# A fixed order of 218 dense chains and a new set of 82 split exponentials in an attention and state-space kernel

## The chip, the cores and the metric

The kernel runs on one core of a Trainium2 chip. The metric is device time in microseconds (us) of one execution. One execution of each kernel is recorded by the profiler; the others are only timed.

A "burst" is one of 512 equal attention steps, and its length is the time from the start of its first exponential on ScalarE to the start of the next burst's first. I compare sums over bursts 17 to 510.

## The reference, cut to what matters

```python
x = A_x                                          # 2048 tokens x 1024
g = sigmoid((x * gate_w).sum(-1, keepdims=True))
a = state_space(x, ...)                          # h[t] = Lam*h[t-1] + B x[t];  y = 2 Re(C h) + x * Dskip
b = attention(x, wqkv, wo)                       # 32 heads of 32, softmax over 2048 keys
return g * a + (1 - g) * b
```

## The kernel before

The two branches run through each other. The attention is the frame: bursts of eight score matmuls, two exponentials of 128x1024 and some sixteen 33-column matmuls of the attention-value product for earlier bursts. Everything else on TensorE (projections "p", state-space inputs "u", state-space outputs "c", the output product "o") is cut into 218 chains that accumulate in one PSUM bank, number 7. A chain has mostly 8 or 16 units, a unit being one 512-column matmul or its like; a burst takes four units. A python function lays the program out once, at build time, and keeps its own rough clock for that.

In some bursts (the set `DVB`) the first exponential is split: ScalarE does a 128x512 half, VectorE the other half in five operations (exp_a to exp_f). I call these bursts "halves".

```python
DVB_FROM = 69
DVB_NOT = (69, 73, 77, ..., 389, 457)           # cut: 34 numbers
DVB = {B for B in range(69, 508) if B % 4 == 1 and B not in DVB_NOT}      # 76 halves (condensed)

def exp(self, B, z, s):
    ...
    if z == 0 and B in DVB:
        self.dve_exp(B, s, p)                    # ScalarE 128x512, VectorE exp_a now, exp_b to exp_f queued in self.dx
    else:
        self.act(lambda e: e.activation(self.tile[p], ps[:, 2 * s:2 * s + 2, :], ACT.Exp, scale=SCALE), ...)

# score buffers: three pairs of PSUM banks in turn
sl = [(2 * self.p) % 3, (2 * self.p + 1) % 3]

# attention-value quarters (four matmuls each) that a burst may take
cap = 5
if p in DVB or p + 1 in DVB:
    cap = 3

# units of dense work in burst p
quota = 3 if p in DVB else 5 if p + 1 in DVB and ... else 4      # condensed

# the next chain: a greedy choice (cut to its core)
if n_ok and left <= need + 4:        cur = nxt.pop(0)            # projection that is due
elif c_ok and ...:                   cur = cs.pop(0)[1]
elif u_ok:                           cur = us.pop(0)[3]
elif c_ok:                           cur = cs.pop(0)[1]
elif n_ok:                           cur = nxt.pop(0)

# a state-space output chain: 16 units, plus four 128x128 matmuls that count as 0 units
for q in range(4):
    mms.insert(5 * q + 3, (0, lambda e, f, l, ...: e.matmul(ps[:, 7, 128 * q:128 * (q + 1)], xT[...], self.diagD[:, dt, :], ...)))

# VectorE's queue: exponential operations first, one after the other
def fill(self, limit):
    while True:
        for src in (self.dx, self.bg, self.bg2):
            ...
```

## Time and profile before

931.95 us, median of 3 (931.95 to 932.35); the profiled execution spans 930.6 us. The busy table of the page (busy us, share of the span, instructions; PE is TensorE's matmuls, PEld its weight loads, DVE VectorE, ACT ScalarE, POOL GpSimd):

```profile
PE 916.7 (99%) x15316; PEld 528.4 (57%) x15316; DVE 733.3 (79%) x1349; ACT 914.9 (98%) x1034; POOL 8.9 (1%) x39
```

Two engines seem full. TensorE's busy time does not tell where it sets the pace: in a stretch that ScalarE paces, shown below, TensorE is busy 29.30 of 29.33 us. (The records of its matmuls overlap: one of 512 columns lasts 0.38 us, and the next of its chain starts 0.215 us after it.) The chain of waits shows which of the two sets the pace where. The first fence is a piece of it between bursts 150 and 152, among halves in every fourth burst; the columns are start, duration and what (L1651 scores, L1725 attention-value, L1481 and L1487 a state-space output chain).

```profile
285.05 0.33 PE f_ps L1651 x8
285.38 0.60 PE f_ps L1725 x20
285.98 0.66 PE f_ps L1481 x3
286.64 0.06 PE f_ps L1487
286.70 0.22 PE f_ps L1481
286.91 0.33 PE f_ps L1651 x8
```

The second is from a stretch without halves (bursts 273 to 288).

```profile
506.71 0.87 PE f_ps L1452 x4
507.58 0.46 PE f_ps L1651 x8
508.04 0.30 PE f_ps L1725 x8
508.34 0.87 PE f_ps L1452 x4
509.21 0.19 PE f_ps L1725 x8
509.41 0.47 PE f_ps L1651 x8
```

In the first, eight score matmuls take 0.33 us and TensorE goes straight from one thing to the next: TensorE paces, and the trace has the first exponential of each burst from 145 to 160 starting about 40 ns after its scores end (from 273 to 288 it is 71 ns or more in 14 of 16 bursts). In the second the same eight take 0.46 us: they wait in the middle for a score buffer that ScalarE has not yet emptied (by the timeline the first such group begins at 507.51 and its third matmul at 507.65, the exponential that reads this buffer having ended at 507.60; the view of waits has 1.7 us of `PEld f_ps L1651 <- ACT f_pt L1667` in bursts 273 to 288 and none in 145 to 160). ScalarE paces. The windows view shows the two kinds side by side; I chose the windows to begin and end at the start of a burst's first exponential, 16 bursts each (145 to 160 first, then 273 to 288), and the column to read is the first number, the length.

```profile
276.83:305.25 28.42, 28.42 (x470) 15.75 (x467) 25.13 (x43) 28.35 (x33) 0.00 (x0) 1.00 0.13 44
500.72:530.05 29.33, 29.30 (x514) 18.35 (x515) 28.02 (x49) 29.33 (x33) 0.27 (x2) 1.00 0.20 43
```

| what (start to next start, or a fit over bursts where the exponential waits for its scores) | us |
|---|---|
| exponential 128x1024 on ScalarE: best, and mean where ScalarE paces | 0.903, 0.917 |
| half exponential 128x512 on ScalarE | 0.494 |
| scores and fixed part of a burst on TensorE (fit) | 0.502 |
| one 33-column matmul, one 512-column, one 128-column (fit) | 0.024, 0.208, 0.053 |
| VectorE, 512 columns, reading the result of the operation before / not reading it | 0.725 / 0.603 |

Over bursts 17 to 510 (8124 33-column, 1735 512-column and 1024 128-column matmuls, 76 halves) the values of the table give TensorE 858 us of work and ScalarE 861 us at its best, and the trace has 878.2 us.

### The profile page before, as it was taken

What the parts mean: (1) busy time and instruction counts of PE and PEld (TensorE: products, weight loads), DVE (VectorE), ACT (ScalarE), POOL (GpSimd) and SP (SyncE); (2) the same over time, 40 slices, a digit from 0 to 9 for tenths busy, and PEclk for the clock granted to TensorE, in tenths of its full rate; (3) what the DMA queues carried; (4) which work ended last, traced back from release to release, by engine and by line L of the source; (5) the groups of instructions that cost most, each with busy time, mean ns of one, the idle gap of its engine ahead of it and who ended that gap; (6) DMA issues with size and microseconds to landing.
All of it is one profiled execution on the core that took longest, in us unless ns stands there. A gap on an engine that the chain in (4) does not pass through costs nothing.

```text
span 930.6 us, 33709 instructions
## 1 busy us (share of the span) xinstructions
PE 916.7 (99%) x15316; PEld 528.4 (57%) x15316; DVE 733.3 (79%) x1349; ACT 914.9 (98%) x1034; POOL 8.9 (1%) x39
## 2 busy tenths in 40 slices
PE   8999999999999999999999999999999999999996
PEld 4555755557555565555655755555655556555553
DVE  2799979999988888886699966579889565766775
ACT  6999999999999999999999999999999999999996
POOL 2000000000000000000000000000000000000000
PEclk9999999999999999999999999999999999999998
DMA  9559433310431004101033201233110212233322
GB/s 204 104 84 154 79 53 76 73 30 5 87 62 42 30 6 86 52 29 31 19 73 63 43 16 56 62 62 72 32 41 8 73 53 93 100 87 123 116 64 75
DMA packets 157076, 60.90 MB, mean 65 GB/s; under 512 B 145664, under 2 KB 145664, under 8 KB 156928
## 3 DMA queue, kind: packets, MB, share of 16 engines
q1 hardware_dynamic: 154768, 58.16, 28.0%
q8 instruction: 121, 1.98, 0.9%
q10 hardware_dynamic: 2160, 0.53, 0.3%
q14 instruction: 27, 0.22, 0.1%
HBM read 16.79 MB, written 12.58 MB: 32 GB/s over the span
## 4 chain that ended last, share of the span: by engine, by line
PE 61%; ACT 36%; DVE 1%; SPq 1%; DMA 1%; issue 0%; DVEq 0%
ACT f_pt L1667 32%; PE f_ps L1725 17%; PE f_ps L1651 13%; PE f_ps L1452 9%; PE f_ps L1481 9%; PE f_ps L1422 8%; PE f_ps L1440 4%; ACT f_ub L1692 1%; SPq L1076 1%; ACT f_wb L1692 1%; DMA f_xT<-in_A_x_dram 1%; ACT f_Et L1667 1%; ACT f_cT_re L1667 1%; PE f_ps L1487 1%; ACT f_cT_im L1667 0%
## 5 line engine op out<-in xcount | busy, mean ns | idle before, releaser
L1667 ACT ACTIVATE f_pt<-f_ps 128x1024 bf16<-128x1024 f32 x868 | 817.7, 1227 | 0.6 <-PE f_ps L1651 0.6
L1725 PEld LDWEIGHTS f_ps<-f_V,f_pt 128*128 128x128 bf16 x6944 | 240.4, 96 | 136.0 <-issue 97.6
L1725 PE MATMUL f_ps<-f_V,f_pt 128*128 128x33 bf16 x6944 | 293.7, 178 | 0.0
L1651 PE MATMUL f_ps<-f_Q,f_K 32*128 32x256 bf16 x4096 | 225.5, 274 | 3.4 <-ACT f_cT_re L1667 1.2
L1651 PEld LDWEIGHTS f_ps<-f_Q,f_K 32*128 32x128 bf16 x4096 | 75.6, 92 | 120.2 <-ACT f_pt L1667 53.5
L1452 PE MATMUL f_ps<-f_xT,f_wb 128*128 128x512 bf16 x512 | 131.0, 377 | 0.9 <-DVE f_pf L1247 0.6
L1422 PE MATMUL f_ps<-f_xT,f_wb 128*128 128x512 bf16 x464 | 119.0, 378 | 0.0
L1371 DVE TENSOR_TENSOR_SCAN f_ht<-f_pf,f_init,f_ut 128x512 bf16<-128x512 f32 x64 | 80.6, 1273 | 0.0
L1481 PE MATMUL f_ps<-f_cT_im,f_hp 128*128 128x512 bf16 x192 | 72.6, 378 | 0.0
L1481 PE MATMUL f_ps<-f_cT_re,f_hp 128*128 128x512 bf16 x192 | 72.5, 378 | 0.0
L1693 DVE TENSOR_SCALAR f_wb<-f_ps 128x512 int32<-128x512 f32 x47 | 32.5, 691 | 49.1 <-PE f_ps L1651 48.7
L1512 PE MATMUL f_ps<-f_wb,f_OT 128*128 128x512 bf16 x252 | 65.9, 380 | 0.0
L1440 PE MATMUL f_ps<-f_wb,f_xT 128*128 128x128 bf16 x896 | 59.1, 219 | 0.0
L1452 PEld LDWEIGHTS f_ps<-f_xT,f_wb 128*128 128x128 bf16 x512 | 40.2, 96 | 32.4 <-issue 0.7
L1422 PEld LDWEIGHTS f_ps<-f_xT,f_wb 128*128 128x128 bf16 x464 | 36.2, 96 | 28.2
L1440 PEld LDWEIGHTS f_ps<-f_wb,f_xT 128*128 128x128 bf16 x896 | 50.4, 97 | 0.1
L1458 DVE CAST f_ub<-f_ps 128x512 bf16<-128x512 f32 x48 | 33.0, 687 | 14.6 <-PE f_ps L1452 14.3
L1363 DVE TENSOR_TENSOR f_tq<-f_ht,f_Et 128x1024 bf16<-128x1024 bf16 x64 | 42.0, 684 | 0.2
L1363 DVE TENSOR_TENSOR f_ut<-f_tq 128x512 f32<-128x512 bf16 x64 | 41.9, 683 | 0.0
L1494 DVE TENSOR_SCALAR f_Ag<-f_ps,f_gcol 128x512 f32<-128x512 f32 x32 | 24.0, 751 | 13.0 <-PE f_ps L1481 12.6
L1700 DVE SCALAR_TENSOR_TENSOR f_Ag<-f_Ag,f_wb 128x512 f32<-128x512 f32 x47 | 32.5, 691 | 1.4
L1692 ACT ACTIVATE f_wb<-f_ps 128x512 bf16<-128x512 f32 x47 | 33.3, 709 | 0.2
(160 smaller groups left out, 937.7 us busy)
## 6 DMA issues: line engine op xcount, KB each, us to landing
ag_scratch<-f_Ag SPq DMA_DIRECT2D x32, 256.0 KB, 2.4
f_hp<-ag_scratch SPq DMA_DIRECT2D x32, 256.0 KB, 3.0
f_wb<-in_B_wqkv_dram SPq DMA_DIRECT2D x21, 256.0 KB, 3.7
out_dram<-f_xT SPq DMA_DIRECT2D x16, 256.0 KB, 2.1
f_wb<-in_B_wo_dram SPq DMA_DIRECT2D x1, 1024.0 KB, 5.3
f_OT<-f_On SPq DMA_TRANSPOSE x63, 2.3
f_wb<-in_B_wo_dram SPq DMA_DIRECT2D x1, 768.0 KB, 6.6
f_wb<-in_B_wqkv_dram ACTq DMA_DIRECT2D x2, 256.0 KB, 4.1
```

The lines of the kernel that those rows point to most:

```text
L1363: ops.append((c, lambda: dve(lambda e: e.tensor_tensor(o, a, b, op), r, w() if callable(w) else w)))
L1371: ops.append((1.192, lambda ri=ri: dve(lambda e: e.tensor_tensor_scan(ht[:, ri, :], rr, ut[:, ri, :], self.init[:, ri, j:j + 1], ALU.mult, ...
L1422: mms.append((1, lambda e, f, l, a=a: e.matmul(ps[:, bank, :], w[:, g % 2, part, a, :], xT[:, a, 512 * ch:512 * (ch + 1)], start=f, stop=l ...
L1440: m = e.matmul(ps[:, bank, 128 * q:128 * (q + 1)], xT[:, a, 128 * kt:128 * (kt + 1)], w[:, g % 2, 2, a, :], start=(a == 0), stop=(a == 7))
L1452: mms.append((1, lambda e, f, l, a=a: e.matmul(ps[:, 7, :], bT[:, n % 2, ri, a, :], xT[:, a, 512 * ch:512 * (ch + 1)], start=f, stop=l), [ ...
L1458: self.dve(lambda e: e.tensor_copy(self.ub[k][:, ri, :], ps[:, 7, :]), [("bank", 7)], [("ub", k, ri)] + over, "evac_u")
L1481: mms.append((1, lambda e, f, l, j=j, ri=ri: e.matmul(ps[:, 7, :], hp[:, ri, j, cols], cT[ri][:, j, 512 * cb:512 * (cb + 1)], start=f, sto ...
L1512: mms.append((1, lambda e, f, l, j=j: e.matmul(ps[:, 7, :], OT[:, j, 256 * qb + 128 * r:256 * qb + 128 * (r + 1)], wo[j][0][:, 512 * cb:51 ...
L1651: m = e.matmul(ps[:, 2 * sl[z] + h % 2, 256 * kl:256 * (kl + 1)], K[32 * h:32 * h + 32, g % 2, 128 * kt:128 * (kt + 1)], Q[32 * h:32 * h + ...
L1667: self.act(lambda e: e.activation(self.tile[p], ps[:, 2 * s:2 * s + 2, :], ACT.Exp, scale=SCALE), [("S", s)], [("pt", p)], "exp")
L1692: self.S.op("act", lambda e: e.activation(t[:, 0, :], ps[:, 2 * s, :], ACT.Exp, scale=SCALE), reads=[("S", s)], writes=[("pt", p)], deps=d ...
L1725: m = e.matmul(ps[:, 6, o:o + 33], self.tile[p][:, h2, 256 * kl + 128 * qt:256 * kl + 128 * (qt + 1)], V[:, g % 2, 2 * i + kl, h, :], star ...
```

## The change

The intent: let a search on a timing model choose the order of all dense chains and the set of halves together, and write both down as lists. To make room on VectorE, exponential operations are interleaved with others (a dependent operation then does not follow its source directly), and some small VectorE operations become fewer and larger.

```diff
-DVB_FROM = 69
-DVB_NOT = (69, 73, 77, ... 457)
+ORDER = "".join(w[0] * int(w[1:]) for w in (
+    "u2 p2 u4 p1 u2 p2 u2 p9 u8 p1 ... p1 c1 p2 c1 p2 c1 p1 u4 c1 u2 p1 c1 p2 c1 u2 p4 c1 p2 c1 u2 p3 ..."   # cut
+    "... p9 c5 p1 c3 u4 ... u2 p9 c8 p3 o36 ").split())
+DVB_RUNS = ((109, 113), (129, 177), (185, 257), (277, 277), (285, 329), (345, 345), (365, 381), (389, 453), (461, 505))
+DVB = {B for lo, hi in DVB_RUNS for B in range(lo, hi + 1, 4)}
...
-                    if n_ok and left <= need + 4:
-                        cur = nxt.pop(0)
-                    elif ...                                     # the greedy choice, cut
+                    kind = order[0]
+                    ...                                          # is the next one of this kind ready?
+                    if not ok:
                         break
+                    order.pop(0)
+                    cur = take()
...
-            for src in (self.dx, self.bg, self.bg2):
+            for src in self.sources():
...
+        if self.dx:
+            out.insert(1 if self.last_dx and self.p < self.dx_due else 0, self.dx)
...
 # fold of C: 64 operations of 512 columns become 32 of 1024; tables: 32 products become 16;
 # the copy of a scan's last column moves behind two other operations
```

The set gains 109, 113, 129, 133, 257, 277, 285, 345, 381, 389 and loses 181, 269, 353, 361: 76 halves become 82.

More of the change, by code (lines that the diff above doesn't have):

```diff
@@ L936 @@
 MM_PER_PERIOD = 4
+UB4 = 16
+DEP = 0.122
 EXP_A = 16713.9646930418
@@ L941 @@
 EXP_C0 = 3607248267949745.0
-DVB_FROM = 69
-DVB_NOT = (69, 73, 77, 81, 85, 89, 93, 97, 101, 105, 109, 113, 117, 121, 125, 129, 133, 257, 261, 265, 273, 277, 281, 285, 333, 337, 341, 345, 349, 357, 381, 385, 389, 457)
-def dve_bursts():
-    return [B for B in range(DVB_FROM, 508) if B % 4 == 1 and B not in DVB_NOT]
-DVB = set(dve_bursts())
+ORDER = "".join(w[0] * int(w[1:]) for w in (
+    "u2 p2 u4 p1 u2 p2 u2 p9 u8 p1 u1 p1 u1 p1 u1 p1 u1 p1 u1 p1 u1 p1 c1 p2 c1 p2 c1 p1 u4 c1 u2 p1 c1 p2 c1 u2 p4 c1 p2 c1 u2 p3 u2 c2 u1 c6 u1 p12 u4 "
+    "p1 u2 p1 u4 p9 c5 p1 c3 u4 p1 u2 p1 u2 p1 u4 p1 u2 p8 u2 p9 c8 p3 o36 ").split())
+DVB_RUNS = ((109, 113), (129, 177), (185, 257), (277, 277), (285, 329), (345, 345), (365, 381), (389, 453), (461, 505))
+DVB = {B for lo, hi in DVB_RUNS for B in range(lo, hi + 1, 4)}
 REST = 508
@@ L1315, in diag_d, with fold_ops @@
                       ["ident", ("pf", 3)], [("diagD", j)])
-    def fold_ops(self, j, cb):
+    def fold_ops(self, j):
         pf = self.pf
         a1, a2, b2 = pf[:, self.A1, j:j + 1], pf[:, self.A2, j:j + 1], pf[:, self.B2, j:j + 1]
-        X, Y = self.fold[:, 0:512], self.fold[:, 512:1024]
-        cols = slice(512 * cb, 512 * cb + 512)
-        cr, ci = self.cT[0][:, j, cols], self.cT[1][:, j, cols]
+        X, Y = self.fold[:, 0:1024], self.fold[:, 1024:2048]
+        cr, ci = self.cT[0][:, j, :], self.cT[1][:, j, :]
         q = lambda *i: [("pf", k) for k in i]
-        gp = ["gp%d" % i for i in range(4)] if j == cb == 0 else []
-        return [(0.4, lambda: self.dve(lambda e: e.tensor_scalar(X, ci, a2, None, ALU.mult), [("cT", 1, j)] + q(self.A2), ["fX"] + gp)),
-                (0.4, lambda: self.dve(lambda e: e.tensor_scalar(Y, cr, a2, None, ALU.mult), [("cT", 0, j)] + q(self.A2), ["fY"])),
-                (0.66, lambda: self.dve(lambda e: e.scalar_tensor_tensor(cr, cr, a1, X, ALU.mult, ALU.add), [("cT", 0, j), "fX"] + q(self.A1), [("cTf", 0, j, cb)])),
-                (0.66, lambda: self.dve(lambda e: e.scalar_tensor_tensor(ci, ci, b2, Y, ALU.mult, ALU.add), [("cT", 1, j), "fY"] + q(self.B2), [("cTf", 1, j, cb)])),
+        gp = ["gp%d" % i for i in range(4)] if j == 0 else []
+        return [(0.66, lambda: self.dve(lambda e: e.tensor_scalar(X, ci, a2, None, ALU.mult), [("cT", 1, j)] + q(self.A2), ["fX"] + gp)),
+                (0.66, lambda: self.dve(lambda e: e.tensor_scalar(Y, cr, a2, None, ALU.mult), [("cT", 0, j)] + q(self.A2), ["fY"])),
+                (1.196, lambda: self.dve(lambda e: e.scalar_tensor_tensor(cr, cr, a1, X, ALU.mult, ALU.add), [("cT", 0, j), "fX"] + q(self.A1), [("cTf", 0, j)])),
+                (1.196, lambda: self.dve(lambda e: e.scalar_tensor_tensor(ci, ci, b2, Y, ALU.mult, ALU.add), [("cT", 1, j), "fY"] + q(self.B2), [("cTf", 1, j)])),
                 (0.0, lambda: self.folded.append(j))]
@@ L1335, in table_ops @@
         EF, Et, prod = self.EF, self.Et, self.fold.rearrange("p (k a b) -> p k a b", k=4, a=32)
-        lo = [EF[:, r, 16 * j:16 * (j + 1)].unsqueeze(1).to_broadcast([128, 32, 16]) for r in range(2)]
-        hi = [EF[:, r, 128 + 32 * j:160 + 32 * j].unsqueeze(2).to_broadcast([128, 32, 16]) for r in range(2)]
+        lo = EF[:, :, 16 * j:16 * (j + 1)].unsqueeze(2).to_broadcast([128, 2, 32, 16])
+        lor = EF[:, ::-1, 16 * j:16 * (j + 1)].unsqueeze(2).to_broadcast([128, 2, 32, 16])
+        hi = EF[:, :, 128 + 32 * j:160 + 32 * j].unsqueeze(3).to_broadcast([128, 2, 32, 16])
         first = ["m_a0", "m_a1", "m_a2", "m_k", "m_h", "m_y", "m_s"] if j == 0 else []
@@ L1341, in table_ops @@
         ops = []
-        for k, (x, y) in enumerate(((0, 0), (1, 1), (0, 1), (1, 0))):
-            ops.append((0.6, lambda k=k, x=x, y=y: self.dve(lambda e: e.tensor_tensor(prod[:, k], hi[x], lo[y], ALU.mult), self.EFtok, ["gp%d" % k] + (first if k == 0 else []))))
+        for k, y in ((0, lo), (2, lor)):
+            ops.append((1.136, lambda k=k, y=y: self.dve(lambda e: e.tensor_tensor(prod[:, k:k + 2], hi, y, ALU.mult), self.EFtok,
+                                                         ["gp%d" % k, "gp%d" % (k + 1)] + (first if k == 0 else []))))
         for r, op in ((0, ALU.subtract), (1, ALU.add)):
@@ L1372, in item_ops @@
                                                 [("ut", ri), "init", ("pf", self.RR)], [("ht", ri)])))
+        tt(0.602, tq[:, 0:2, :], ht[:], E2, ALU.mult, [("ht", 0), ("ht", 1), Et], [("tq", 0)])
+        tt(0.602, tq[:, 2:4, :], ht[:], E2r, ALU.mult, [("ht", 0), ("ht", 1), Et], [("tq", 2)])
         if ch < 3:
             ops.append((0.19, lambda: dve(lambda e: e.tensor_copy(self.hl[:, :, j], ht[:, :, 511]), [("ht", 0), ("ht", 1)], [("hl", j)])))
-        tt(0.602, tq[:, 0:2, :], ht[:], E2, ALU.mult, [("ht", 0), ("ht", 1), Et], [("tq", 0)])
-        tt(0.602, tq[:, 2:4, :], ht[:], E2r, ALU.mult, [("ht", 0), ("ht", 1), Et], [("tq", 2)])
         hw = ["warm"] if ch == 0 and j == 0 else []
@@ L1466, in ub_of @@
     def ub_of(self, n):
-        return n % 4 if n < 16 else n % 2
+        return n % 4 if n < UB4 else n % 2
     def done_item(self, n):
@@ L1481, in d_c @@
                 mms.append((1, lambda e, f, l, j=j, ri=ri: e.matmul(ps[:, 7, :], hp[:, ri, j, cols], cT[ri][:, j, 512 * cb:512 * (cb + 1)], start=f, stop=l),
-                            [("hp", b, j, ri), ("cTf", ri, j, cb)]))
+                            [("hp", b, j, ri), ("cTf", ri, j)]))
         for q in range(4):
@@ L1697, in dve_exp @@
         self.waiting.add(B)
-        self.dx += [(0.45, lambda: self.dve(lambda e: e.tensor_scalar(hi, hi, 0.0, 128.0, ALU.max, ALU.mult), [I], [I], "exp_b")),
-                    (0.69, lambda: self.dve(lambda e: e.scalar_tensor_tensor(xw, lo, EXP_C2, lo, ALU.add, ALU.mult), [I], [W], "exp_c")),
-                    (0.69, lambda: self.dve(lambda e: e.scalar_tensor_tensor(xw, xw, EXP_C1, lo, ALU.add, ALU.mult), [I, W], [W], "exp_d")),
-                    (0.69, lambda: self.dve(lambda e: e.scalar_tensor_tensor(t[:, 1, :], xw, EXP_C0, ev, ALU.add, ALU.mult), [I, W], [("ptd", p)], "exp_f")),
+        self.last_dx, self.dx_due = True, B + 3
+        self.dx += [(0.365, lambda: self.dve(lambda e: e.tensor_scalar(hi, hi, 0.0, 128.0, ALU.max, ALU.mult), [I], [I], "exp_b")),
+                    (0.603, lambda: self.dve(lambda e: e.scalar_tensor_tensor(xw, lo, EXP_C2, lo, ALU.add, ALU.mult), [I], [W], "exp_c")),
+                    (0.603, lambda: self.dve(lambda e: e.scalar_tensor_tensor(xw, xw, EXP_C1, lo, ALU.add, ALU.mult), [I, W], [W], "exp_d")),
+                    (0.603, lambda: self.dve(lambda e: e.scalar_tensor_tensor(t[:, 1, :], xw, EXP_C0, ev, ALU.add, ALU.mult), [I, W], [("ptd", p)], "exp_f")),
                     (0.0, lambda: self.waiting.discard(B))]
@@ L1745, in normalize @@
             if g == 3:
-                assert self.items_done >= 16
+                assert self.items_done >= UB4
                 x += [("ub", k, ri) for k in (2, 3) for ri in range(2)]
@@ L1762, in build @@
         self.holds, self.left_in = {}, {}
+        self.last_dx, self.dx_due = False, 0
         self.dx, self.seen_x, self.waiting, self.x_now, self.busy_w = [], set(), set(), None, None
@@ L1791, in build @@
                 for tq in range(4):
-                    cs.append((ch, self.d_c(ch, tq, cb, len(cs)), 8 + 8 * cb))
+                    cs.append((ch, self.d_c(ch, tq, cb, len(cs))))
         self.c_left = [8, 8, 8, 8]
@@ L1807, in build @@
         cur = None
+        order = list(ORDER)
         first = FIRST
@@ L1840, in build @@
                 self.normalize(nq // 32 - 1)
+                self.last_dx = False
                 self.dve_t = max(self.dve_t, rn) + 0.6
@@ L1845, in build @@
                 if nc == 8:
-                    for cb in range(2):
-                        for j in range(8):
-                            self.bg2 += self.fold_ops(j, cb)
+                    for j in range(8):
+                        self.bg2 += self.fold_ops(j)
             while self.later and self.later[0][0] <= p:
@@ L1878, in build @@
                 if cur is None:
-                    if ended is not None:
+                    if ended is not None or not order:
                         break
-                    if proj[0] and p >= FIRST + 4:
-                        cur = proj[0].pop(0)
-                    elif not last:
-                        nxt = proj[g + 1]
-                        left = 64 - pg
-                        need = 2 * len(nxt)
-                        u_ok = c_ok = False
-                        if us:
-                            ch, n, ri, dn = us[0]
-                            hp_free = ch < 2 or (ch == 2 and self.c_left[0] == 0) or (ch == 3 and self.c_left[2] == 0)
-                            u_ok = ri == 1 or (self.items_done >= n - (3 if n < 18 else 1) and hp_free)
-                        if cs:
-                            c_ok = self.items_done >= 8 * (cs[0][0] + 1) and p > self.item_p + 1 and len(self.folded) >= cs[0][2]
-                        n_ok = nxt and pg >= nxt[0].after
-                        if n_ok and left <= need + 4:
-                            cur = nxt.pop(0)
-                        elif c_ok and cs[0][0] == 1 and p + 4 * sum(self.c_left[:2]) + need >= 254:
-                            cur = cs.pop(0)[1]
-                        elif u_ok:
-                            cur = us.pop(0)[3]
-                        elif c_ok:
-                            cur = cs.pop(0)[1]
-                        elif n_ok:
-                            cur = nxt.pop(0)
-                    elif outs and p >= outs[0][0]:
-                        cur = outs.pop(0)[1]
@@ L1907, in build @@
-                    if cur is None:
+                    kind = order[0]
+                    if kind == "p":
+                        if proj[0]:
+                            ok, src = p >= FIRST + 4, proj[0]
+                        else:
+                            src = proj[g + 1] if g + 1 < GROUPS else None
+                            ok = src and pg >= src[0].after
+                        take = lambda: src.pop(0)
+                    elif kind == "u":
+                        ch, n, ri, dn = us[0]
+                        hp_free = ch < 2 or (ch == 2 and self.c_left[0] == 0) or (ch == 3 and self.c_left[2] == 0)
+                        ok = ri == 1 or (self.items_done >= n - (3 if n < UB4 + 2 else 1) and hp_free)
+                        take = lambda: us.pop(0)[3]
+                    elif kind == "c":
+                        ok = self.items_done >= 8 * (cs[0][0] + 1) and p > self.item_p + 1 and len(self.folded) == 8
+                        take = lambda: cs.pop(0)[1]
+                    else:
+                        ok = last and p >= outs[0][0]
+                        take = lambda: outs.pop(0)[1]
@@ L1935, in build @@
                 ended.evac()
+                self.last_dx = False
                 st = max(self.dve_t, ready)
@@ L1939, in build @@
         self.log = log
-        assert not outs and cur is None and nq == 4 * NBURST - 8
+        self.missing = sum(w for w in [dn.left for dn in [cur] if dn]) + sum(dn.left for l in (us, cs, outs) for dn in [t[3] if len(t) == 4 else t[1] for t in l])
+        assert not self.missing and nq == 4 * NBURST - 8
         self.tail()
@@ L1945, in fill @@
         while True:
-            for src in (self.dx, self.bg, self.bg2):
-                if not src:
-                    continue
-                if src is self.bg:
-                    n = src[0][2]
-                    if n < 8 and n not in self.tabled or n >= 8 and len(self.folded) < 16:
-                        continue
-                if src is self.bg2 and len(src[0]) > 2 and self.p < src[0][2]:
-                    continue
+            for src in self.sources():
                 c = src[0][0]
+                if src is self.dx and self.last_dx:
+                    c += DEP
                 if c == 0 or self.dve_t + c <= limit:
@@ L1958, in fill @@
                     self.dve_t += c
+                    if c:
+                        self.last_dx = src is self.dx
                     break
@@ L1961, in fill, with sources @@
                 return
+    def sources(self):
+        out = []
+        for src in (self.bg, self.bg2):
+            if not src:
+                continue
+            if src is self.bg:
+                n = src[0][2]
+                if n < 8 and n not in self.tabled or n >= 8 and len(self.folded) < 8:
+                    continue
+            if src is self.bg2 and len(src[0]) > 2 and self.p < src[0][2]:
+                continue
+            out.append(src)
+        if self.dx:
+            out.insert(1 if self.last_dx and self.p < self.dx_due else 0, self.dx)
+        return out
     def tail(self):
```

## The prediction

> **What bounds the kernel now.** The busy table shows TensorE 99%, ScalarE 98%, VectorE 79%, clock 0.996. [...] I read the rhythm of the exponentials in the timeline. A burst gives ScalarE two 128x1024 exponentials; in 76 bursts the first is a 128x512 half (start to next start 0.49 us), VectorE doing the other half.
>
> - In stretches without halves (bursts 65 to 128, 257 to 288, 337 to 352) ScalarE paces: 29.33 us per 16 bursts, 0.917 us per exponential, 0.903 at best. A fit of burst lengths where ScalarE waits for the scores puts TensorE's work there at 27.5 to 28.0 us (about 0.50 us of scores, 0.024 us per 33-column matmul, 0.208 us per 512-column matmul): 1.3 to 1.8 us spare per 16.
> - With one half in every four bursts (145 to 256, 305 to 332, 401 to 432) TensorE paces: each exponential starts about 40 ns after its scores end; 16 bursts take 27.5 to 28.4 us where ScalarE needs 27.3.
>
> Over bursts 17 to 510 both engines' own work is near 860 us, the measured time 878. The bounds alternate; the loss is the alternation. VectorE is nearly full only from 40 to 240 us (17 to 19.7 us busy per 20 in the windows).
>
> **What the change does.** The instruction order shows the same TensorE work (1964 dense units) and tail. Halves go from 76 to 82: added at 109, 113, 129, 133, 257, 277, 285, 345, 381, 389, removed at 181, 269, 353, 361. Most added ones lie where ScalarE paces, each worth 0.92 - 0.49 = 0.42 us; 181 cost nothing to drop; 353 and 361 cost up to 0.8 together. Chains move slightly: the excess of 145 to 160 (68 units) drops to 66, and goes to 113 to 128, which has room.
>
> VectorE gains 6 x 3.1 us of exponential work. It saves more: a dependent 512-column operation starts 0.725 us after its source operation, an independent one 0.603; interleaving hides up to some 170 such bubbles (20 us, estimated); the fold at 1024 columns saves about 4 us, the tables 1, the moved 2-column copy 2 to 3. VectorE is not on the path (1% of the chain of waits), so these only make room for the six.
>
> **On the critical path.** Taking for each stretch the larger of TensorE's fitted work and ScalarE's measured pace, the sum falls by 2.6 to 3.3 us for stretches of 4 to 32 bursts. Fewer late evictions may give another 0 to 2 us. Opening and tail stay. So 931.95 - 3.7 = 928.2 us, 8 in 10 within 925.3 to 930.8: within 2%.
>
> **In the profile after:** 82 half exponentials and 942 full; bursts 113 to 144 shorter by 1.2 to 1.8 us together, 273 to 288 by 0.7 to 0.8, 353 to 368 longer by 0.2 to 0.8, and 161 to 256 and 401 to 432 nearly unchanged; VectorE's busy time within 10 us of 733; TensorE's busy time 912 to 916 us.
>
> **What would make this wrong.** Interleaving may bring the last exponential operation or an eviction late, so that TensorE waits on VectorE: a loss of some us, seen as waits on VectorE. Or the losses that I took as fixed (mostly 0.3 to 0.7 us per 16 bursts over the larger bound) come from VectorE's lateness and go away: 923 to 925 us.

The savings given for VectorE, and the 0 to 2 us for fewer late evictions, were estimates. The two traces put the fold at 4.1 us (start to start 0.396 and 0.662 us for its operations of 512 columns, 0.664 and 1.195 for those of 1024) and the tables at 1.1 us (32 operations of 0.602, 16 of 1.135). They do not show the 2 to 3 us for the moved copy: where the same operations follow a scan, the one after them starts 2.589 us after the scan in both kernels. The five operations of a half last 3.2 us together, and VectorE is busy 17.4 to 19.7 us in nine of the ten windows from 40 to 240 us, but 15.6 in 120 to 140.

## The result, and the profile after

928.85 us, median of 4 (928.26 to 930.74), against 932.15 us for the kernel before in the same rounds. The ratio is 0.9968 with a 95% interval of 0.995 to 0.9985. Ratios here and below are the mean time of one kernel's runs over that of the other's of the same rounds, so not quite the ratio of the medians. The verdict is "same" by the 2% rule; the gain is small and real. The profiled execution, of 928.26 us, spans 926.5 us.

```profile
PE 892.4 (96%) x15095; PEld 525.4 (57%) x15316; DVE 737.3 (80%) x1331; ACT 911.3 (98%) x1034; POOL 8.9 (1%) x39
```

TensorE's busy time must not be read as a gain of 24 us: 221 of 15316 matmul records are missing (the weight loads beside them are complete). Traces of close variants that have all records show 911 to 913 us.

The two windows, now 145 to 160 and 273 to 288 in the changed kernel:

```profile
274.94:302.75 27.81, 27.31 (x454) 15.12 (x459) 24.36 (x44) 27.81 (x33) 0.00 (x0) 1.00 0.14 38
498.39:526.99 28.60, 28.13 (x504) 17.94 (x508) 25.59 (x46) 28.60 (x33) 0.00 (x0) 1.00 0.24 44
```

The group lines of the half exponentials (one line of the split exponential on ScalarE for each place where VectorE's scratch lies; only the largest is shown, before and then after; x is their number): six more.

```profile
L1692 ACT ACTIVATE f_wb<-f_ps 128x512 bf16<-128x512 f32 x47 | 33.3, 709 | 0.2
```

```profile
L1691 ACT ACTIVATE f_wb<-f_ps 128x512 bf16<-128x512 f32 x53 | 38.4, 725 | 0.1
```

Lengths of the stretches of 16 bursts that moved by 0.25 us or more, in us, with the number of halves in brackets:

| bursts | before | after | difference | foreseen |
|---|---|---|---|---|
| 97 to 112 | 29.33 (0) | 29.02 (1) | -0.31 | |
| 113 to 128 | 29.33 (0) | 28.94 (1) | -0.40 | 113 to 144 together |
| 129 to 144 | 28.80 (2) | 27.76 (4) | -1.04 | -1.2 to -1.8 |
| 145 to 160 | 28.42 (4) | 27.81 (4) | -0.61 | shorter |
| 177 to 192 | 27.51 (4) | 27.89 (3) | +0.38 | nothing |
| 273 to 288 | 29.33 (0) | 28.60 (2) | -0.73 | -0.7 to -0.8 |
| 337 to 352 | 29.10 (0) | 28.65 (1) | -0.45 | |
| 353 to 368 | 28.20 (3) | 28.97 (1) | +0.76 | +0.2 to +0.8 |
| 369 to 384 | 27.88 (3) | 27.63 (4) | -0.25 | |
| 385 to 400 | 28.69 (2) | 28.16 (3) | -0.54 | |
| 17 to 510, sum | 878.24 | 874.52 | -3.72 | -3.7 |

So the time is right to 0.7 us and most stretches are where they were expected. That does not yet say why. Three things changed together (set, order, interleaving), and each could be the cause.

### The profile page after: what moved, and what is told of

Read it like the earlier page. It is cut to its first block, busy times and chain, and to the rows that moved or that the text cites. A ratio compares the mean times of both kernels' runs of the same rounds, so it can differ in the third digit from the quotient of the medians.

```text
span 926.5 us, 33493 instructions
## 1 busy us (share of the span) xinstructions
PE 892.4 (96%) x15095; PEld 525.4 (57%) x15316; DVE 737.3 (80%) x1331; ACT 911.3 (98%) x1034; POOL 8.9 (1%) x39
## 3 DMA queue, kind: packets, MB, share of 16 engines
q1 hardware_dynamic: 154768, 58.16, 28.3%
## 4 chain that ended last, share of the span: by engine, by line
PE 55%; ACT 37%; DVE 5%; issue 1%; SPq 1%; DMA 1%; DVEq 0%
ACT f_pt L1666 33%; PE f_ps L1725 16%; PE f_ps L1650 11%; PE f_ps L1480 8%; PE f_ps L1451 8%; PE f_ps L1421 8%; PE f_ps L1439 4%; SPq L1074 1%; ACT f_ub L1691 1%; ACT f_wb L1691 1%; DVE f_ht L1370 1%; DMA f_xT<-in_A_x_dram 1%; ACT f_Et L1666 1%; ACT f_cT_re L1666 1%; PE f_ps L1486 1%
## 5 line engine op out<-in xcount | busy, mean ns | idle before, releaser
L1650 PE MATMUL f_ps<-f_Q,f_K 32*128 32x256 bf16 x4096 | 220.9, 273 | 4.2 <-ACT f_pt L1666 1.2
L1650 PEld LDWEIGHTS f_ps<-f_Q,f_K 32*128 32x128 bf16 x4096 | 72.7, 92 | 118.4 <-ACT f_pt L1666 63.4
L1451 PE MATMUL f_ps<-f_xT,f_wb 128*128 128x512 bf16 x448 | 117.4, 377 | 8.2 <-issue 2.1
L1421 PE MATMUL f_ps<-f_xT,f_wb 128*128 128x512 bf16 x406 | 106.7, 378 | 4.5 <-issue 0.5
L1692 DVE TENSOR_SCALAR f_wb<-f_ps 128x512 int32<-128x512 f32 x53 | 36.6, 691 | 52.4 <-PE f_ps L1650 52.3
L1511 PE MATMUL f_ps<-f_wb,f_OT 128*128 128x512 bf16 x218 | 57.8, 378 | 3.0 <-issue 0.2
L1480 PE MATMUL f_ps<-f_cT_re,f_hp 128*128 128x512 bf16 x147 | 55.5, 378 | 0.2
L1691 ACT ACTIVATE f_wb<-f_ps 128x512 bf16<-128x512 f32 x53 | 38.4, 725 | 0.1
L1701 DVE SCALAR_TENSOR_TENSOR f_wb<-f_Ag,f_wb 128x512 bf16<-128x512 f32 x53 | 36.5, 689 | 1.2
L1700 DVE SCALAR_TENSOR_TENSOR f_Ag<-f_Ag,f_wb 128x512 f32<-128x512 f32 x53 | 36.3, 685 | 0.7
```

The lines of the kernel that those rows point to most:

```text
L1421: mms.append((1, lambda e, f, l, a=a: e.matmul(ps[:, bank, :], w[:, g % 2, part, a, :], xT[:, a, 512 * ch:512 * (ch + 1)], start=f, stop=l ...
L1451: mms.append((1, lambda e, f, l, a=a: e.matmul(ps[:, 7, :], bT[:, n % 2, ri, a, :], xT[:, a, 512 * ch:512 * (ch + 1)], start=f, stop=l), [ ...
L1480: mms.append((1, lambda e, f, l, j=j, ri=ri: e.matmul(ps[:, 7, :], hp[:, ri, j, cols], cT[ri][:, j, 512 * cb:512 * (cb + 1)], start=f, sto ...
L1511: mms.append((1, lambda e, f, l, j=j: e.matmul(ps[:, 7, :], OT[:, j, 256 * qb + 128 * r:256 * qb + 128 * (r + 1)], wo[j][0][:, 512 * cb:51 ...
L1650: m = e.matmul(ps[:, 2 * sl[z] + h % 2, 256 * kl:256 * (kl + 1)], K[32 * h:32 * h + 32, g % 2, 128 * kt:128 * (kt + 1)], Q[32 * h:32 * h + ...
L1691: self.S.op("act", lambda e: e.activation(t[:, 0, :], ps[:, 2 * s, :], ACT.Exp, scale=SCALE), reads=[("S", s)], writes=[("pt", p)], deps=d ...
```

## The experiments

My theory: a half is worth the difference of the two exponentials, 0.42 us, where ScalarE paces, and next to nothing where TensorE paces; the order is worth a little; the interleaving, being on an engine off the path, is worth nothing by itself and only makes room. Rivals: the interleaving is the cause, through earlier evictions; or the order is; or ScalarE's total counts, wherever a half lies.

First, what could not be run. The kernel's builder has assertions of its own (for instance, that the state-space work is done before its buffers are reused). The kernel before with the new set of halves does not build, with or without the interleaving; nor does the changed kernel with the greedy order, with the old set, or with its full set and no interleaving. The parts need each other to fit, which says nothing of what each is worth. So each was tested beside a partner with the same reduced set.

### What a half is worth, by place

```diff
 DVB = {B for lo, hi in DVB_RUNS for B in range(lo, hi + 1, 4)}
+DVB = DVB - {345, 277, 285} | frozenset()        # e_minus_act3
+DVB = DVB - {217, 313, 421} | frozenset()        # e_minus_pe3
+DVB = DVB - frozenset() | {457}                  # e_plus457
```

> The changed kernel without the halves at bursts 277, 285 and 345, which lie where ScalarE paces (79 halves left); list, interleaving and merges kept. Theory (a half is worth 0.42 us where ScalarE paces, the gain is the set of halves): bursts 273 to 288 take 29.3 to 29.5 us again (28.6 in the changed kernel), 337 to 352 29.0 to 29.2 (28.65), all others stay within 0.15; the whole kernel is 1.0 to 1.4 us slower than the changed one. Rival (the gain comes from the interleaving and the evictions that come earlier by it): these stretches change by less than 0.4 us together.

Measured: 929.64 us, ratio to the kernel before 0.9981 (0.9967 to 0.9995). In the trace 273 to 288 grow from 28.60 to 29.41, 337 to 352 from 28.65 to 29.05, other stretches by at most 0.04; 1.26 us in all over bursts 17 to 510, 0.42 for each half. The theory holds here.

> The changed kernel without the halves at bursts 217, 313 and 421, which lie where every exponential starts some 40 ns after its scores end (79 halves left). Theory (TensorE paces there, a half is worth nearly nothing): bursts 209 to 224, 305 to 320 and 417 to 432 grow by 0 to 0.2 us each, 0 to 0.5 us together. Rival A (ScalarE's total is what counts, wherever a half lies): 0.42 us each, 1.27 us together, as in the run without 277, 285 and 345. Rival B: the pace is set burst by burst with little elasticity, so that four bursts without a half take ScalarE's 7.33 us instead of some 7.02: 0.3 us each, 0.9 us together.

Measured: 929.26 us, ratio 0.9974 (0.996 to 0.9987). 209 to 224 grow by 0.39, 305 to 320 by 0.43, of which 0.25 comes back in 321 to 336, 417 to 432 by 0.29: 0.86 us in all, 0.29 for each half. That is rival B's total (0.9), and neither the theory's (at most 0.5) nor rival A's (1.27). My theory fails here: in these stretches nearly every burst's first exponential had been waiting for TensorE (46 of 48), and over 16 bursts TensorE's work in 209 to 224 (28.3 us by the fit, 28.06 by the trace) exceeds or equals ScalarE's even with three halves (27.7 to 28.1 us, at 0.903 and 0.917). Still a half was worth two thirds of the full amount.

Rival B's reason, that four bursts without a half take ScalarE's 8 x 0.917 = 7.33 us, is not shown. Bursts 217 to 220 and 221 to 224, in the changed kernel and then without the half at 217:

```profile
400.50:407.52 7.02, 6.89 (x118) 3.87 (x120) 4.34 (x10) 7.02 (x10) 0.00 (x0) 1.00 0.16 49
407.52:414.54 7.02, 6.89 (x118) 3.87 (x120) 3.89 (x7) 7.02 (x10) 0.00 (x0) 1.00 0.11 41
```

```profile
400.45:407.98 7.53, 7.51 (x125) 4.04 (x125) 1.39 (x5) 7.51 (x9) 0.00 (x0) 1.00 0.14 46
407.98:414.89 6.91, 6.91 (x116) 3.76 (x116) 3.88 (x6) 6.91 (x9) 0.00 (x0) 1.00 0.11 40
```

The four bursts take 7.53 us, more than ScalarE's 7.33, and the next four give 0.11 back. At 313 it is 7.53 too, and at 421 7.34. The edit does more than remove a half: where a half goes, `cap` and the quota change, and the builder moves attention-value matmuls. Burst 217 gets 24 of them, where the fit gives TensorE 1.96 us and the trace has 1.96. How much of the 0.29 us is ScalarE's pace and how much TensorE's moved work, no run separates; that cause stays open.

> The changed kernel with one half more, at burst 457 (83 halves), in bursts 449 to 464, where ScalarE paces with three halves (27.99 us) and the fit of TensorE's work says 26.7. Theory: this stretch falls by 0.3 to 0.45 us, nothing else moves by more than 0.15. Rival (the output chains that begin at 459 make TensorE or VectorE pace there): no change or slower.

Measured: 927.66 us, ratio 0.9957 (0.9944 to 0.9971). 449 to 464 fall by 0.25 and 465 to 480 by 0.16, in all by 0.42 us; nothing else moves by more than 0.02. The total is as the theory has it, the place is not (0.3 to 0.45 named for the first stretch, at most 0.15 elsewhere): only 0.19 us is gained in the half's own four bursts, the rest in the 20 bursts after them. Relief in one burst is thus carried on well beyond four. The timed ratio, 0.9957 against the changed kernel's 0.9968, points the same way, but these intervals overlap.

### The interleaving alone, on either side

The first of three kernels is the kernel before with the interleaving; the other two are the changed kernel without the halves at 185, 285 and 401, with the interleaving off and on. In the first, the costs of these operations in the builder's clock change too (cut here).

```diff
-            for src in (self.dx, self.bg, self.bg2):              # e_inter_only, from the kernel before
+            for src in self.sources():
```

```diff
-            out.insert(1 if self.last_dx and self.p < self.dx_due else 0, self.dx)
+            out.insert(0, self.dx)                                # e_nointer79; e_inter79 keeps the old line
+DVB = DVB - {185, 285, 401} | frozenset()                         # both
```

> The kernel before with the interleaving of the exponential operations alone (and its costs in the builder's clock); old set of 76 halves, old greedy order, old fold and table widths. Theory (interleaving only makes room on VectorE, which is off the path): within 0.7 us of the kernel before, no stretch of 16 bursts shorter by more than 0.3 us. Rival (interleaving brings evictions and the last exponential operation earlier and TensorE waits less): 2 to 4 us faster, spread over the stretches with halves. VectorE's busy time falls by 5 to 20 us in either case.

> The changed kernel with the interleaving taken out (the exponential operations of a burst go first and follow each other again), and without the halves at 185, 285 and 401, without which the list of chains no longer builds (79 halves). To be compared with the run that drops the same three and keeps the interleaving. Theory (interleaving only makes room): over bursts 17 to 510 the two differ by less than 0.5 us; VectorE's busy time is 10 to 20 us longer here. Rival (interleaving shortens waits on VectorE): this one is 2 us or more longer.

> The changed kernel without the halves at 185, 285 and 401, interleaving kept (79 halves). From the first four runs: 285 lies where ScalarE paces and costs 0.41 us; 185 and 401 lie among halves in every fourth burst and cost about 0.28 each as 217, 313 and 421 did on average; together 0.9 to 1.1 us more than the changed kernel over bursts 17 to 510.

Measured: 929.75 us without it (ratio 0.9978, 0.9964 to 0.9991) and 929.54 us with it (0.9977, 0.9963 to 0.999). Over bursts 17 to 510 the traces have 875.74 and 875.67 us: with set and order fixed, the interleaving is worth 0.07 us. The three halves cost 1.15 us (0.39, 0.39 and 0.36 in the three stretches), a little over the 0.9 to 1.1 expected. VectorE's busy lines, without it and with it:

```profile
PE 913.2 (98%) x15316; PEld 526.2 (57%) x15316; DVE 735.2 (79%) x1316; ACT 912.4 (98%) x1034; POOL 9.2 (1%) x39
```

```profile
PE 913.0 (98%) x15316; PEld 526.1 (57%) x15316; DVE 729.7 (79%) x1316; ACT 912.3 (98%) x1034; POOL 8.9 (1%) x39
```

It saves 5.5 us of VectorE's time, not 10 to 20: the trace has 185 pairs of exponential operations that follow each other directly with a gap of 30 to 40 ns without it and still 128 with it.

In the kernel before it even cost something: 933.11 us, ratio 1.0012 (0.9998 to 1.0025, so the timed runs alone do not show it), and 878.92 us against 878.24 in the trace. No stretch was shorter by more than 0.14. The loss sat in a few stretches, most of it in 401 to 432, which went from 56.10 to 56.65 us. That was not in the theory, and it led to the next experiment.

### Where 0.55 us came from: the phase of the chains

In 401 to 432 both kernels do nothing but "c" chains, four bursts each, with a half in every fourth burst (but for the last two to four bursts). What differs is where a chain ends: in the half's own burst in the kernel before, two bursts ahead of a half with the interleaving (scan items are finished at other moments, so the greedy choice takes a projection chain after the c chains and not before). TensorE's timeline at such a change of chain with the interleaving (L1482 is the chain; the last line is the first matmul of the next):

```profile
739.69 0.38 PE L1482 MATMUL f_ps<-f_cT_im,f_hp 128*128 128x512 bf16 x1
739.90 0.26 PE L1727 MATMUL f_ps<-f_V,f_pt 128*128 128x33 bf16 x4
740.01 0.25 PE L1727 MATMUL f_ps<-f_V,f_wb 128*128 128x33 bf16 x4
740.19 0.40 PE L1652 MATMUL f_ps<-f_Q,f_K 32*128 32x256 bf16 x8
740.52 0.47 PE L1727 MATMUL f_ps<-f_V,f_pt 128*128 128x33 bf16 x12
740.91 0.39 PE L1482 MATMUL f_ps<-f_cT_re,f_hp 128*128 128x512 bf16 x1
```

And VectorE's, the eviction of bank 7 (in brackets its idle time before and what ended it):

```profile
740.10 0.75 DVE L1495 TENSOR_SCALAR f_Ag<-f_ps,f_gcol 128x512 f32<-128x512 f32 x1 [1.26 <-PE f_ps L1482]
```

VectorE is idle for 1.26 us before and starts at once when the chain ends, so it is not late. The eviction ends at 740.85, and the next chain's first matmul starts 0.06 us later. Between the chains TensorE has only 8 attention-value matmuls, the scores and 12 more (`cap` is 3 in the burst ahead of a half), which do not quite cover 0.75 us. After a half's own burst there are 4 and 20, and they do. The remedy in the next kernel is one condition:

```diff
                         n_ok = nxt and pg >= nxt[0].after
+                        if 395 <= p < 397:
+                            c_ok = False
```

> The run with the interleaving alone, with one line more: at bursts 395 and 396 no output chain of the state-space part may be started, so that one value-projection chain (two bursts) comes before the 32 bursts of such chains instead of after them, as in the kernel before. Interleaving and the set of halves are the same. Theory (a chain's eviction of 0.75 us is covered only by the scores and the attention-value matmuls between two chains; two bursts ahead of a half there are 12 of these and not 20, so a chain that ends there costs TensorE 0.07 to 0.09 us): bursts 401 to 432 fall from 56.65 us to 56.0 to 56.2, and the excess of the interleaving over the kernel before (0.7 us over bursts 17 to 510) falls to 0 to 0.2. Rival (the interleaving delays evictions on VectorE there): 401 to 432 stay above 56.5.

Measured: 401 to 416 take 28.07 us and 417 to 432 take 28.03, together 56.10 as in the kernel before, and the sum over bursts 17 to 510 falls from 878.92 to 878.33. (In this trace 449 to 464 are 0.17 us longer than in both others, with the same matmuls; the cause is not shown.) 932.52 us, ratio 0.9999 (0.9985 to 1.0012). (This trace lacks 221 matmul records, so I show the same phase in the kernel before, whose trace is whole.) TensorE first, then VectorE:

```profile
742.96 0.38 PE L1481 MATMUL f_ps<-f_cT_im,f_hp 128*128 128x512 bf16 x1
743.18 0.26 PE L1725 MATMUL f_ps<-f_V,f_pt 128*128 128x33 bf16 x4
743.37 0.40 PE L1651 MATMUL f_ps<-f_Q,f_K 32*128 32x256 bf16 x8
743.70 0.37 PE L1725 MATMUL f_ps<-f_V,f_pt 128*128 128x33 bf16 x8
743.91 0.25 PE L1725 MATMUL f_ps<-f_V,f_wb 128*128 128x33 bf16 x4
744.01 0.35 PE L1725 MATMUL f_ps<-f_V,f_pt 128*128 128x33 bf16 x8
744.22 0.38 PE L1481 MATMUL f_ps<-f_cT_re,f_hp 128*128 128x512 bf16 x1
```

```profile
743.38 0.75 DVE L1494 TENSOR_SCALAR f_Ag<-f_ps,f_gcol 128x512 f32<-128x512 f32 x1 [0.32 <-PE f_ps L1481]
```

The eviction again begins as soon as the chain has ended and takes 0.75 us, to 744.13, but now the next chain's turn comes only at 744.22. From the start of the last attention-value matmul to that of the chain's first it takes 0.025 us here and 0.10 us in the other phase.

A chain that ends in the wrong phase thus costs about 0.08 us (seven of them, 0.55 us). The kernel before has four such chains in 145 to 160: that stretch takes 28.42 us there, while 401 to 416, with the same matmuls in each burst and the other phase, takes 28.07.

### The order alone

The full set does not build with the greedy choice, so both kernels drop 129, 277, 285, 345, 381 and 389; one keeps the list, one has the old choice put back.

```diff
+DVB = DVB - {129, 277, 285, 345, 381, 389} | frozenset()     # both
-                    kind = order[0]                              # e_greedy76 only: the greedy choice again
+                    if proj[0] and p >= FIRST + 4: ...
```

> The changed kernel with the old greedy choice of chains in place of the list, and 76 halves: without 129, 277, 285, 345, 381 and 389, because the greedy choice does not build with the full set. To be compared with the next run, which has the same 76 halves and the list. Theory (the order of chains is worth little by itself: it levels 145 to 160): 0.3 to 0.9 us longer over bursts 17 to 510, most of it in bursts 129 to 176. Rival (the order is where the gain comes from): 2 us or more longer, spread.

> The changed kernel with its list and without the halves at 129, 277, 285, 345, 381 and 389 (76 halves, as many as the kernel before). Theory: 129, 277, 285 and 345 cost 0.41 us each, 381 and 389 0.25 to 0.41 each: 2.1 to 2.5 us longer than the changed kernel over bursts 17 to 510, so about 1.3 us shorter than the kernel before.

Measured: greedy 933.19 us (ratio 1.0008, 0.9995 to 1.0022), list 931.09 us (0.9992, 0.9978 to 1.0006). In the trace 878.57 and 877.01: the order is worth 1.56 us, between what I gave it (0.3 to 0.9) and the rival's 2 or more. 0.57 of it is in 145 to 160 as expected, but 0.68 is in 401 to 432, where I expected nothing: the phase of the chains again (seven "c" chains of the greedy kernel end two bursts ahead of a half there, none of the list's). Of these 0.68 us only 0.13 is a gain over the kernel before, which has the good phase there (56.10 us, the list's kernel 55.97): the list mostly repairs what the interleaving spoils under the greedy choice. The list with 76 halves is 1.23 us faster than the kernel before with its 76, and the six halves are worth 2.49 us, 0.42 each.

### The small matmuls that count as nothing

A "c" chain carries four 128x128 matmuls that the units do not count. A list that mixes such chains with others spreads them. Here they are left out everywhere, so the result is wrong on purpose (relative error 0.58), with every other instruction in its place.

```diff
+            elif wt == 0:
+                pieces.append((0, lambda: None))
```

> The changed kernel without the four 128x128 matmuls of each output chain of the state-space part (they add the skip term, so the result is wrong on purpose); all else is in the same place. The fit gives each 0.053 us, 0.21 us a chain, 6.8 us for all 32. Theory (they cost time only where TensorE paces, which is why moving such chains to stretches where ScalarE paces gains): 209 to 224 and 417 to 432 fall by 0.5 to 0.85 us each, 113 to 128 (two such chains) by less than 0.2; 2.5 to 4.5 us in all over bursts 17 to 510. Rival (ScalarE paces everywhere once there are four halves in 16 bursts): below 1.5 us in all.

Measured: 926.07 us, ratio 0.9926 (0.991 to 0.9941), and 2.51 us less over bursts 17 to 510, at the lower edge of what I expected. 209 to 224 fall by 0.49 and 417 to 432 by 0.44, just under the 0.5 named, 113 to 128 by 0.05; other stretches grow, 337 to 352 most (0.26). So these matmuls are paid for where chains of this kind stand close together among halves and nearly free elsewhere; of the 6.8 us of the fit, about a third is on the path. The rest falls on ScalarE's pace: with them gone, stretches with four halves stop at 27.6 us.

### Two lists made from these terms

A random search over lists and sets, judged by the larger of TensorE's fitted work and ScalarE's pace over every two and every four bursts, with exposed evictions counted, gave two kernels with 86 halves.

```diff
-    "u2 p2 u4 p1 u2 p2 u2 p9 u8 p1 u1 p1 ...
+    "u2 p2 u3 p1 u1 p1 u2 p1 u1 p5 u1 p6 u2 p2 ... c1 p1 u1 p1 u1 c1 u1 p1 c1 p2 ... c3 p2 c3 p1 c1 o36"     # e_best86a, cut
-DVB_RUNS = ...
+DVB = {77, 81, 89, 113, 129, 137, ..., 505}                                             # cut
```

> The changed kernel with another list and 86 halves, found by small random moves judged by this sum: for every two and every four bursts the larger of TensorE's fitted work (with an exposed eviction counted where few matmuls stand between two chains) and ScalarE's pace. Halves are added at 77, 81, 89, 181, 261, 265, 269, 273, 333, 337, 357, 385 and 457 and removed at 109, 133, 185, 277, 293, 369, 377, 393 and 401; output chains of the state-space part are mixed with the others all along. Theory (these terms are what the time is made of): 2.0 to 2.8 us less than the changed kernel over bursts 17 to 510. Rival (the terms hold only near the kernels they were read from, and with 86 halves VectorE, full between 40 and 240 us, delays evictions and exponentials): less than 1 us gained, with waits of TensorE on VectorE.

> The same search from another start, also 86 halves (added 77, 85, 93, 181, 261, 265, 269, 273, 333, 337, 341, 353, 385, 457; removed 109, 173, 189, 277, 289, 345, 369, 373, 389, 397). Theory: 1.9 to 2.7 us less than the changed kernel over bursts 17 to 510. Rival: less than 1 us.

Measured: 927.26 us (ratio 0.995, 0.9936 to 0.9963) and 927.08 us (0.9953, 0.9939 to 0.9967); 873.42 and 873.52 us in the trace, 1.10 and 1.00 us less than the changed kernel. Less than the theory's range, and next to the rival's (less than 1 us). In both nearly the whole shortfall is in one place: 445 to 448 take 8.23 us in the first of them and 6.81 in the changed kernel. The view of waits, in that part of the first:

```profile
DVE f_xT L1519 <- DMA f_hp<-ag_scratch: 1.8, 1, 1.8
...
PEld f_ps L1513 <- DVE f_xT L1519: 1.4, 1, 1.4
PE f_ps L1513 <- DVE f_xT L1519: 1.3, 1, 1.3
```

The first output chain's eviction adds a state-space tile that has been to HBM and back (in this window the store, `ag_scratch<-f_Ag`, takes 2.0 us from issue to landing and a reload, `f_hp<-ag_scratch`, 3.2 in the median), and both lists end "c1 o36": the last state-space chain comes right before the outputs, so the reload is late: VectorE waits 1.8 us for it, and TensorE 1.3 for the eviction. That is a wait on VectorE, as the rival had it, but VectorE waits for the DMA there and is not full. The changed kernel's list has three projection chains in between. My sum had no term for this. Without these 1.42 us the first list would have gained 2.52 us, inside the range; that is arithmetic, no run. All three (the two lists and the one with 457) beat both given kernels in the trace; the timed runs tell them apart neither from each other nor, by their intervals, from the changed kernel.

## Why the prediction was right

The predicted time, 928.2 us, is 0.65 us under the measured median of 928.85, and the range of 925.3 to 930.8 holds it. Point by point:

- **The two paces and their places: right.** Where ScalarE paces, a half gains 0.42 us (277, 285, 345 and 457), as 0.92 - 0.49 said.
- **"181 cost nothing to drop": wrong.** 177 to 192 grew by 0.38 us. The step that failed is taking TensorE's pace there as proof that a half is free: for 177 to 192 of the kernel before, the fit gives TensorE 27.5 us and ScalarE needs 27.3 with four halves, but 27.7 to 28.1 with three. TensorE's lead was smaller than the 0.42 us of a half, and ScalarE paces once it is gone. The greedy kernel, with the same numbers of matmuls but without 181, takes 27.93 us there, against 27.48 with it (`e_inter_only`, which lacks the merges too). Even in the fullest TensorE-paced stretches three halves were worth 0.29 each, where the larger of the two sums said 0; that cause stays open.
- **353 and 361 "up to 0.8 together": right**, at 0.76.
- **"Chains move slightly": too little.** The order is worth 1.56 us at a common set, 0.68 of it mostly the repair named above. The excess of 145 to 160 was seen; the eviction that shows between two chains was not, and it is part of what I took as fixed loss and thought might be VectorE's lateness. VectorE was idle there; the time is the eviction's own 0.75 us behind too few matmuls.
- **Interleaving off the path: right** (0.07 us). Its size on VectorE was not: 5.5 us and 57 gaps, not some 170 and 20 us. VectorE's busy time, 737.3 us, is within the 10 us of 733 that I gave.
- **TensorE's busy time 912 to 916 us:** not testable on this trace, which lacks 221 records; 911 to 913 in variants with all of them, so at the lower edge.

The sum was right partly by luck: a removed half that cost 0.38 us and an order that gave more than I allowed nearly cancel. The two paces alone had given 2.6 to 3.3 us; the rest of the 3.7 was an allowance for fewer late evictions through the interleaving, which is worth 0.07 us. What came in its place, as far as the steps below show, was the order. In a table of steps, all over bursts 17 to 510:

| step | us | difference |
|---|---|---|
| before (76 halves, greedy) | 878.24 | |
| greedy, interleaving and merges, 76 halves of the new set | 878.57 | +0.33 |
| the list in place of the greedy choice | 877.01 | -1.56 |
| six more halves: after | 874.52 | -2.49 |

About 60% of what the last two steps gain is halves and 40% order; against the kernel before the share of the order is smaller, since the first step contains the loss of 0.55 us in 401 to 432 that the list repairs. The merges alone were not run; they are in the first step.

## What to carry to other kernels

When two engines take turns in setting the pace, the larger of two sums over a stretch is only a first estimate of its time: take one piece of relief out of a stretch where it should be free before it is called free (0.29 us each here, not 0), and check what else the edit moves. Of the 1.56 us from order alone, at most 0.57 lies where the list mixes "c" chains with others (145 to 160), and 0.68 is a matter of whether an engine's eviction hides behind the other's work. When a change is smaller than the spread of the runs, compare the lengths of fixed pieces of the trace instead: they repeat to 0.02 us here while whole executions differ by 2.5 us.

## What the traces showed beside the answer

- A sum over 16 bursts (28 us) said 0 for a half among its like, and the run says 0.29 us; an added half gained 0.19 us in its own four bursts (7 us) and 0.23 in the 20 after them.
- This kernel has one bank for all its chains, and the cost can be named: 0.08 us per change of chain where scores and 20 short matmuls stand between two chains, none that showed with scores and 24 of them, for an eviction of 0.75 us.
- An operation of 512 columns on VectorE that reads its predecessor's result starts 0.725 us after it, one that does not 0.603 us. Its own record lasts about 0.69 us: in the first case 0.034 us lie between the two records, in the second they overlap by 0.08.
- Merging two fold operations of 512 columns (0.662 us each, start to start) into one of 1024 (1.195) saved 0.13 us. It is not so for all operations: the independent ones of 0.603 us leave some 0.07 us beside the 0.53 that 512 columns add here (1.195 - 0.662; an estimate from these figures).
